# One core, attention and two mixing layers: the DMA order within a head pair laid out by phase, and the E value products moved one slot later

## The chip, the core and the metric

One core of a Trainium2 chip. The metric is the device time of one launch in microseconds (us); the time of the kernel before is the median of three runs. A profiled execution of the same kernel gives the trace.

## What is computed

Three stages follow each other; only the first is touched by the change. The inputs are float32, with 4 batches, 8 heads, 1152 keys, 576 pooled queries and a head dimension of 64.

```python
q_pool = q.reshape(B, H, S // 2, 2, D).mean(axis=3)
scores = scale * np.matmul(q_pool, k.transpose(0, 1, 3, 2))
attn = np.exp(scores - np.max(scores, axis=-1, keepdims=True))
attn = attn / (np.sum(attn, axis=-1, keepdims=True) + 1e-09)
attn_out = np.matmul(attn, v)
# then a gated layer (w_k, w_v, w_r) and a token/channel mixing layer (w_theta, w_tok_*, w_ch)
```

Some weights of the later layers are the bit patterns of 64-bit floats and are turned into pairs of 32-bit numbers by the kernel itself, partly during the attention.

## The kernel before

The 32 heads are handled as 16 pairs (P = 0 to 15). A pair has nine tiles of up to 128 queries against 1152 keys, so there are 144 slots; slot 9P + t belongs to tile t of pair P. The main loop (line 615) runs over the slots. In each slot s it emits, in this order, the entries of `gaps`, the softmax work of tiles s and s+1, the entries of `mids`, the score products and row maxima of tile s+2, the value products planned for s (`run_pv`), and the entries of `sched` (registered by `at`). Each engine and the DMA-issuing queue of SyncE (SP) run what they were given in this order and wait where data are missing; an emission slot is therefore an order and not a time. In one slot, entries of the same list run in the order of their registration: normalisation and block moves first, then `prep_sched`, then the weight conversion.

In pairs 1 to 14 (`quick`) tiles 0 to 3 are transposed in 32x32 blocks by VectorE into `BLK` (line 359), and `move_blocks` (line 361) then puts the blocks in place with 16 DMAs of 32 partitions by 4608 bytes from `BLK` to `E` (line 368), 2.36 MB in a pair. Tiles 4 to 8 are transposed by TensorE (line 334) and copied to `M` (line 391). `pv_part` (line 406) multiplies the values with E (group 0, 18 matmuls, two instructions each) and with M (group 1). Which slots do this is in `shares` (line 340): group 0 in slots 7, 8 and 9 of a pair, group 1 in slots 10, 11 and 12, which are slots 1 to 3 of the next pair.

The other things that go on in a pair's slots:
- `prep_sched` (line 486, tables `PREP1` and `PREP`) prepares the next pair: `kh` and `kl` cut k in two parts on GpSimd (POOL), `km` moves one part by two DMAs of 295 KB (line 255), `q` splits the pooled queries on POOL (`q_split`, line 235), and `lk`, `lq`, `lv` load k, q and v (lines 224, 229, 233; 590 KB for k, for v, and for each half of q).
- `norm1` (line 420) turns the row sums into reciprocals on VectorE, transposes them and stores them to DRAM with four small DMAs (`scr`, line 430); `spread` (line 433) reads them back as a broadcast (`rb`, two DMAs, line 437); `norm2` (line 440) multiplies on POOL. `NORM = (14, 2)` puts norm1 at the end of slot 14, which is slot 5 of the next pair, spread one slot later and norm2 in slot 18.
- The weight conversion (`conv_steps`, line 107): 20 pieces, each a load of 524 KB (line 123), three VectorE steps (`bits`, lines 134, 138 and 142), a few ScalarE and POOL steps, and two stores of 262 KB to DRAM (lines 154, 155). The table `CONV` puts one of the VectorE steps into each of slots 4 to 8 of a pair, and the loads and stores follow seven slots before the first step and three after the last. The pieces rotate through three buffers (`cp`), so the load of one waits for the landing of the stores of the one three before.

SP thus issues everything in one order: the load of a conversion piece stands ahead of the loads of k and q, and these ahead of the 16 block moves. From slot NT = 144 on the later layers run (`mixtures`).

## Time and profile before

| | us |
|---|---|
| median of 3 runs | 1013.45 |
| lowest and highest run | 1011.31, 1016.57 |
| profiled execution, whole | 1010.17 |
| its span, first to last instruction | 1008.4 |
| attention, pairs 1 to 14 (exponential of first tile of pair 1 to that of pair 15) | 446.2 |
| mean granted TensorE clock | 0.978 |

The span is 1.8 us below the profiled execution's time. Times in the rows are us from the start of the span. PE is TensorE, PEld its weight loads, DVE VectorE, ACT ScalarE, SPq the issuing queue of SyncE. In a timeline or a group the bracket or the last column tells how long the engine stood idle before the work and what the profile names as the end of that wait. When several things are waited for, the one that came last is named; the four `scr<-rt` stores are issued right after the 16 block moves, and no matmul reads them, so where a value product is said to have waited for `scr<-rt` it is the E tile that it was waiting for.

### The profile page before, as it was taken

What the parts mean: (1) busy time and instruction counts of PE and PEld (TensorE: products, weight loads), DVE (VectorE), ACT (ScalarE), POOL (GpSimd) and SP (SyncE); (2) the same over time, 40 slices, a digit from 0 to 9 for tenths busy, and PEclk for the clock granted to TensorE, in tenths of its full rate; (3) what the DMA queues carried; (4) which work ended last, traced back from release to release, by engine and by line L of the source; (5) the groups of instructions that cost most, each with busy time, mean ns of one, the idle gap of its engine ahead of it and who ended that gap; (6) DMA issues with size and microseconds to landing.
All of it is one profiled execution on the core that took longest, in us unless ns stands there. A gap on an engine that the chain in (4) does not pass through costs nothing.

```text
span 1008.4 us, 17632 instructions
## 1 busy us (share of the span) xinstructions
PE 935.0 (93%) x6328; PEld 789.0 (78%) x6328; DVE 691.8 (69%) x1006; ACT 517.3 (51%) x1101; POOL 593.0 (59%) x631
## 2 busy tenths in 40 slices
PE   7987997979886988999999999999999999999998
PEld 5765665656564655666779989999999999999998
DVE  6786877876687676877555978888835766466632
ACT  6665654655465455665565555555544434243410
POOL 7846765666565656576622655656646657465731
PEclk9999998999999898999999999999999999999999
DMA  8678978887888788796356333333320701010001
GB/s 213 184 194 220 252 212 238 224 227 212 234 214 219 213 231 229 201 252 165 132 204 215 105 105 91 100 91 106 108 105 7 266 1 48 1 42 7 24 25 48
DMA packets 65848, 150.36 MB, mean 149 GB/s; under 512 B 11936, under 2 KB 31072, under 8 KB 65760
## 3 DMA queue, kind: packets, MB, share of 16 engines
q1 hardware_dynamic: 65760, 149.22, 52.2%
q8 instruction: 50, 0.82, 0.3%
q14 instruction: 38, 0.31, 0.1%
HBM read 81.92 MB, written 24.79 MB: 106 GB/s over the span
## 4 chain that ended last, share of the span: by engine, by line
PE 65%; DMA 13%; DVE 6%; SPq 6%; issue 5%; POOL 3%; ACT 2%; ACTq 0%; POOLq 0%; DVEq 0%
PE ps L1059 11%; PE pv L406 11%; PE sc L291 9%; PE ps L811 9%; PE ps L792 8%; DMA E<-blk 5%; PE ps L1078 5%; PE ps L1005 5%; SPq L368 4%; PE sc L334 3%; PE ps L761 3%; DMA scr<-rt 2%; DMA qn<-qT 2%; DVE m L312 2%; DMA a<-wk 1%
## 5 line engine op out<-in xcount | busy, mean ns | idle before, releaser
L291 PE MATMUL sc<-kt,q 128*128 128x384 f32 (+1 forms) x864 | 204.8, 359 | 25.0 <-DVE M L391 20.3
L324 ACT ACTIVATE e<-sc,m 128x1152 f32<-128x1152 f32 x144 | 176.3, 1225 | 90.0 <-DVE m L312 87.2
L312 DVE TENSOR_REDUCE m<-sc 128x1 f32<-128x1152 f32 x138 | 187.0, 1355 | 49.7 <-PE sc L291 42.9
L291 PEld LDWEIGHTS sc<-kt,q 128*128 128x128 f32 (+1 forms) x864 | 143.1, 188 | 59.2 <-DVE M L391 33.1
L1059 PE MATMUL ps<-b,a 128*128 128x288 f32 x816 | 111.3, 296 | 0.0
L1059 PEld LDWEIGHTS ps<-b,a 128*128 128x128 f32 x816 | 109.4, 189 | 0.6
L406 PE MATMUL pv<-E,vn 128*64 128x256 f32 x576 | 78.9, 413 | 31.6 <-DMA scr<-rt 27.7
L792 PE MATMUL ps<-x,a 128*128 128x288 f32 x768 | 105.2, 298 | 2.3 <-DVE xt L816 2.3
L792 PEld LDWEIGHTS ps<-x,a 128*128 128x128 f32 x768 | 103.8, 191 | 2.6 <-DVE xt L816 2.6
L811 PE MATMUL ps<-k,b 128*128 128x288 f32 x768 | 103.6, 295 | 0.0
L811 PEld LDWEIGHTS ps<-k,b 128*128 128x128 f32 x768 | 102.2, 188 | 0.3
L391 DVE COPY M<-sc 128x384 f32<-128x384 f32 x77 | 41.8, 545 | 72.5 <-PE sc L334 72.4
L201 POOL TENSOR_TENSOR kt<-kn,kh 64x576 fp32r<-64x576 f32 (+1 forms) x64 | 90.1, 1427 | 2.2
L334 PEld LDWEIGHTS sc<-idn,e 128*128 128x128 f32 x528 | 61.3, 147 | 36.5 <-ACT e L324 18.4
L334 PE MATMUL sc<-idn,e 128*128 128x128 f32 x528 | 80.0, 290 | 8.2 <-ACT e L324 7.1
L406 PE MATMUL pv<-M,vn 128*64 128x320 f32 x576 | 87.5, 441 | 0.0
L406 PEld LDWEIGHTS pv<-E,vn 128*64 128x64 f32 x576 | 41.2, 145 | 58.5 <-issue 43.9
L391 ACT COPY M<-sc 128x384 f32<-128x384 f32 x83 | 39.4, 480 | 80.9 <-PE sc L334 80.4
L359 DVE STREAM_TRANSPOSE blk<-e 128x1152 f32<-128x1152 f32 x56 | 76.5, 1367 | 0.0
L779 POOL TENSOR_TENSOR k<-h,k 128x288 fp32r<-128x288 f32 x64 | 56.7, 895 | 28.3 <-ACT k L778 27.0
L150 POOL TENSOR_TENSOR cv<-cv 128x512 fp32r<-128x512 f32 x20 | 25.6, 1278 | 77.1 <-ACT cv L146 63.5
L406 PEld LDWEIGHTS pv<-M,vn 128*64 128x64 f32 x576 | 37.4, 136 | 36.1 <-issue 11.2
(136 smaller groups left out, 1658.3 us busy)
## 6 DMA issues: line engine op xcount, KB each, us to landing
E<-blk SPq DMA_DIRECT2D x224, 144.0 KB
qn<-qT SPq DMA_DIRECT2D x60, 288.0 KB
vn<-vP SPq DMA_DIRECT2D x16, 576.0 KB
kt<-kh SPq DMA_DIRECT2D x31, 288.0 KB
kn<-kT SPq DMA_DIRECT2D x15, 576.0 KB
b<-wtk SPq DMA_DIRECT2D x9, 576.0 KB
rb<-scr SPq DMA_DIRECT2D x32, 144.0 KB
out<-xt SPq DMA_DIRECT2D x32, 144.0 KB
```

The lines of the kernel that those rows point to most:

```text
L201: engines[e].tensor_tensor(out, x, hi.bitcast(F32), ALU.subtract)
L291: r = pe.matmul(sc[0:m, c, 0:384], lhsT=x, rhs=k[:, 384 * c:384 * c + 384], start=(i == 0), stop=(i == len(ops) - 1),)
L312: r = dve.tensor_reduce(m, scs[n][:, :, 0:384], axis=AX.XY, op=ALU.max, negate=True)
L324: r = act.activation(e, sc[:, :, 0:384], AF.Exp, bias=m, scale=1.0, accum_out=rss[P][:, t:t + 1])
L334: r = pe.transpose(ps[:, 128 * j:128 * j + 128], es_[n][:, c, 128 * j:128 * j + 128], idn)
L359: dve.transpose(out, es_[n].rearrange("p a b -> p (a b)").rearrange("p (k m i) -> p k m i", k=KT, m=4))
L391: r = (act.copy if e == "act" else dve.tensor_copy)(out, ps)
L406: pe.matmul(out, lhsT=vns[P][:, h, j], rhs=e, start=(x == 0), stop=(x == KT - 1))
L779: pool.tensor_tensor(q[:, 1], h, q[:, 0].bitcast(F32), ALU.subtract)
L792: pe.matmul(ps, lhsT=WK[k, f // 4][:, w, 128 * (f % 4):128 * (f % 4) + 128], rhs=x[k][:, c], start=(k == 0 and n == 0), stop=(k == 3 and n ...
L811: pe.matmul(pss[d], lhsT=WV[f][:, w, 128 * d:128 * d + 128], rhs=k2[f][:, c], start=(f == 0 and n == 0), stop=(f == 7 and n == 2))
L1059: pe.matmul(pss[d], lhsT=zs[j][z][:, 128 * d:128 * d + 128], rhs=WTK[min(j, 8)][:, w, cs], start=(m == 0 and n == 0), stop=(m == 8 and n = ...
```

## The change

It redistributes work over slots; no arithmetic is removed.
- `shares`: E products in slots 8 (four key tiles) and 9 (five) in place of 7, 8 and 9 (three each); in pair 14 in slots 7 (two) and 8 (seven).
- Normalisation: `NORM = 9`. The two small steps on the sums go to POOL (`norm0`, slot 9), the reciprocal and the transpose to the end of slot 10 (VectorE), the four stores to the middle of slot 11, the read back to the middle of slot 12, the multiplication to the end of slot 14. Slots 9 to 14 are slots 0 to 5 of the next pair. Stores and read back now stand ahead of that pair's block moves.
- Preparation: `km` from slot 0 to the end of slot 1, `lk` from 2 to 1, first half of `lq` from the end of slot 2 to the middle of 3, second half from 7 to 8, `lv` from 7 to 8.
- Conversion: pieces are tied to pairs 1 to 13, two in odd pairs and one in even ones. Loads at the end of the slot before the pair, the VectorE steps in slots 4, 5, 6 and, for the second piece, 6, 7, 8; stores in the middle of slot 2 of the next pair.

```diff
-NORM = (14, 2)
+NORM = 9
-PREP = ((0, 0, 'kh', 'pool'), (0, 2, 'km'), (0, 2, 'q', 0), (2, 2, 'lk'), (2, 2, 'lq', 0), (2, 1, 'kl', 'pool', 0, 0), (2, 2, 'kl', 'pool', 0, 1), (3, 2, 'q', 1), (5, 1, 'kl', 'pool', 1, 0), (5, 2, 'kl', 'pool', 1, 1), (7, 2, 'lq', 1), (16, 2, 'lv'))
-CONV = ((4, 1), (5, 1), (6, 1), (7, 1), (8, 1))
+PREP = ((0, 0, 'kh', 'pool'), (1, 2, 'km'), (0, 2, 'q', 0), (1, 2, 'lk'), (3, 1, 'lq', 0), (2, 1, 'kl', 'pool', 0, 0), (2, 2, 'kl', 'pool', 0, 1), (3, 2, 'q', 1), (5, 1, 'kl', 'pool', 1, 0), (5, 2, 'kl', 'pool', 1, 1), (8, 2, 'lq', 1), (17, 2, 'lv'))
+BITS = ((4, 5, 6), (6, 7, 8))
...
             if P == NP - 2:
-                return ((7, 5), (8, 4)), ((9, 5), (11, 4))
+                return ((7, 2), (8, 7)), ((9, 5), (11, 4))
...
-            return ((7, 3), (8, 3), (9, 3)), ((10, 3), (11, 3), (12, 3))
+            return ((8, 4), (9, 5)), ((10, 3), (11, 3), (12, 3))
...
+        def norm0(P):
+            rs, r2 = rss.pop(P), R2[P % 2]
+            pool.tensor_scalar(r2[:, 0:KT], rs[:, 0:KT], 1e-9, 1.0, op0=ALU.add, op1=ALU.mult)
+            pool.tensor_scalar(r2[0:64, KT:KT + 1], r2[64:128, 4:5], 1.0, 1.0, op0=ALU.mult, op1=ALU.mult)
...
-            dve.tensor_scalar(r2[:, 0:KT], rs[:, 0:KT], 1e-9, 1.0, op0=ALU.add, op1=ALU.mult)
-            dve.reciprocal(r2[:, 0:KT], r2[:, 0:KT])
-            dve.tensor_copy(r2[0:64, KT:KT + 1], r2[64:128, 4:5])
+            dve.reciprocal(r2[:, 0:KT + 1], r2[:, 0:KT + 1])
             dve.transpose(rt, r2)
...
+        def norm3(P):
+            scr, rt = scrs.pop(P)
             for b4 in range(4):
                 sp.dma_start(out=scr[:, 32 * b4:32 * b4 + 32], in_=rt[32 * b4:32 * b4 + KT + 1, :])
-            at(last_slot + 3 if P == NP - 1 else P * KT + NORM[0] + 1, spread, P, scr)
+            (at if P == NP - 1 else at_mid)(last_slot + 3 if P == NP - 1 else P * KT + NORM + 3, spread, P, scr)
...
-            o, hook = NORM
-            (at_gap, at_mid, at)[hook](min(P * KT + o, NT), norm1, P)
-            at(min(P * KT + o, NT) + (4 if P < NP - 1 else 6), norm2, P)
+            at(P * KT + NORM, norm0, P)
+            at(min(P * KT + NORM + 1, NT), norm1, P)
+            at_mid(min(P * KT + NORM + 2, NT + 1), norm3, P)
+            at(P * KT + NORM + (5 if P < NP - 1 else 6), norm2, P)
...
+        for P in range(1, NP - 2):
+            base = P * KT
+            for bits, (i, piece) in zip(BITS[:1 + P % 2], pieces):
...
+                at(base - 1, load)
+                at_mid(base + 2, mag)
+                at(base + 2, clamp)
+                for o, step in zip(bits, cuts):
+                    at_mid(base + o, step)
+                at_mid(base + KT, hi)
+                at(base + KT, lo)
+                at_mid(base + KT + 2, store)
```

## Rows read from the trace of the kernel before

**Rows 1.** The page's second part: busy tenths of TensorE in 40 slices of 25.2 us.

```profile
PE   7987997979886988999999999999999999999998
```

**Rows 2.** Stretches, pairs 1, 5, 9, 12, 14: us; busy PE, PEld, DVE, ACT, POOL; PEclk; DMA; GB/s.

```profile
38.60:67.20 28.60, 25.03 (x163) 18.16 (x160) 24.61 (x30) 17.16 (x31) 16.43 (x16) 1.00 0.63 159
...
166.90:196.00 29.10, 27.12 (x179) 18.92 (x177) 24.48 (x28) 18.69 (x35) 20.25 (x20) 1.00 0.85 240
...
295.30:332.10 36.80, 28.61 (x175) 19.59 (x174) 24.81 (x27) 18.07 (x35) 19.45 (x19) 0.89 0.82 202
...
397.90:427.70 29.80, 27.56 (x179) 19.33 (x178) 24.39 (x28) 17.51 (x34) 18.53 (x17) 0.98 0.80 218
...
455.90:484.80 28.90, 27.71 (x186) 19.23 (x183) 20.52 (x23) 16.57 (x32) 15.80 (x15) 1.00 0.63 157
```

**Rows 3.** Groups by line, whole span: busy, mean ns | idle before, what ended it.

```profile
L406 PE MATMUL pv<-E,vn 128*64 128x256 f32 x576 | 78.9, 413 | 31.6 <-DMA scr<-rt 27.7 <-DMA E<-blk 3.9
```

**Rows 4.** Timeline of PE around slot 7 of pairs 9 and 12.

```profile
328.01 2.83 PE L406 MATMUL pv<-E,vn 128*64 128x256 f32 x12 [5.95 <-DMA scr<-rt]
...
422.13 0.62 PE L291 MATMUL sc<-kt,q 128*128 128x384 f32 x2 [1.55 <-DVE M L391]
...
425.29 1.52 PE L406 MATMUL pv<-E,vn 128*64 128x256 f32 x12
426.73 0.88 PE L334 MATMUL sc<-idn,e 128*128 128x128 f32 x6
...
428.92 1.52 PE L406 MATMUL pv<-E,vn 128*64 128x256 f32 x12
```

**Rows 5.** Timeline of SP's issues in pair 9, up to its block moves.

```profile
299.35 0.54 SPq L155 DMA_DIRECT2D wv<-cv  x1
308.95 0.33 SPq L123 DMA_DIRECT2D cv<-wv  x1
309.33 0.43 SPq L224 DMA_DIRECT2D kn<-kT  x1
309.86 1.13 SPq L229 DMA_DIRECT2D qn<-qT  x2
311.10 13.45 SPq L368 DMA_DIRECT2D E<-blk  x16
```

**Rows 6.** The same in pair 12: block moves, store of sums, read back.

```profile
411.61 10.99 SPq L368 DMA_DIRECT2D E<-blk  x16
422.70 1.58 SPq L430 DMA_DIRECT2D scr<-rt  x4
425.37 1.12 SPq L437 DMA_DIRECT2D rb<-scr  x2
```

**Rows 7.** Waits, us in total, times, longest: three of SP's queue, one of TensorE.

```profile
SPq L368 <- DVE blk L359: 33.1, 7, 10.6
...
SPq L123 <- DMA wk<-cv: 22.7, 4, 8.6
SPq L437 <- DMA scr<-rt: 21.1, 21, 2.4
...
PE pv L406 <- DMA scr<-rt: 27.7, 9, 6.0
```

**Rows 8.** Timeline of VectorE in pair 7.

```profile
238.71 1.36 DVE L312 TENSOR_REDUCE m<-sc 128x1 f32<-128x1152 f32 x1
...
243.54 1.37 DVE L359 STREAM_TRANSPOSE blk<-e 128x1152 f32<-128x1152 f32 x1
...
250.96 0.89 DVE L142 SCALAR_TENSOR_TENSOR cv<-cv 128x512 uint32<-128x512 uint32 x1
...
253.29 0.22 DVE L425 RECIPROCAL r<-r 128x9 f32<-128x9 f32 x1
...
253.72 0.21 DVE L427 STREAM_TRANSPOSE rt<-r 128x32 f32<-128x32 f32 x1
```

**Rows 9.** One stretch of pair 12 ahead of its block moves, columns as in rows 2.

```profile
402.00:406.00 4.00, 4.00 (x28) 2.55 (x28) 3.93 (x4) 2.37 (x5) 3.66 (x5) 1.00 1.02 271
```

More of the change, by code (lines that the diff above doesn't have):

```diff
@@ L29 @@
 HALF = 288
-CFIRST = 4
 WARM = 16
@@ L216, in attention @@
         for t in RS + R2:
-            pool.memset(t, 0.0)
+            pool.memset(t, 1.0)
         for b in range(NB):
@@ L418, in attention @@
         rbs = {}
+        scrs = {}
+        def norm0(P):
+            rs, r2 = rss.pop(P), R2[P % 2]
+            pool.tensor_scalar(r2[:, 0:KT], rs[:, 0:KT], 1e-9, 1.0, op0=ALU.add, op1=ALU.mult)
+            pool.tensor_scalar(r2[0:64, KT:KT + 1], r2[64:128, 4:5], 1.0, 1.0, op0=ALU.mult, op1=ALU.mult)
         def norm1(P):
-            rs = rss.pop(P)
             r2 = R2[P % 2]
             rt = sm.tile([128, 32], F32, tag="rt", name="rt")
-            dve.tensor_scalar(r2[:, 0:KT], rs[:, 0:KT], 1e-9, 1.0, op0=ALU.add, op1=ALU.mult)
-            dve.reciprocal(r2[:, 0:KT], r2[:, 0:KT])
-            dve.tensor_copy(r2[0:64, KT:KT + 1], r2[64:128, 4:5])
+            dve.reciprocal(r2[:, 0:KT + 1], r2[:, 0:KT + 1])
             dve.transpose(rt, r2)
             scr = dram.tile([KT + 1, 128], F32, tag="scr", name="scr")
+            scrs[P] = scr, rt
+        def norm3(P):
+            scr, rt = scrs.pop(P)
             for b4 in range(4):
                 sp.dma_start(out=scr[:, 32 * b4:32 * b4 + 32], in_=rt[32 * b4:32 * b4 + KT + 1, :])
-            at(last_slot + 3 if P == NP - 1 else P * KT + NORM[0] + 1, spread, P, scr)
+            (at if P == NP - 1 else at_mid)(last_slot + 3 if P == NP - 1 else P * KT + NORM + 3, spread, P, scr)
         def spread(P, scr):
@@ L588, in attention @@
             prep_sched(P)
-        places = [(KT * i + o, hook) for i in range(NP - 1) for o, hook in CONV]
-        for i, piece in enumerate(first):
-            load, mag, clamp, *bits, hi, lo, store = conv_steps(lambda i: cp.tile([128, 1536], F32R, tag="cv", name="cv"), piece, i, engines[CLO], pool)
-            mine = places[CFIRST + 3 * i:CFIRST + 3 * i + 3]
-            a, z = mine[0][0], mine[-1][0]
-            at(a - 7, load)
-            at_mid(a - 2, mag)
-            at(a - 2, clamp)
-            for (o, hook), step in zip(mine, bits):
-                (at_gap, at_mid, at)[hook](o, step)
-            at_mid(z + 1, hi)
-            at(z + 1, lo)
-            at(z + 3, store)
+        pieces = iter(enumerate(first))
+        for P in range(1, NP - 2):
+            base = P * KT
+            for bits, (i, piece) in zip(BITS[:1 + P % 2], pieces):
+                load, mag, clamp, *cuts, hi, lo, store = conv_steps(lambda i: cp.tile([128, 1536], F32R, tag="cv", name="cv"), piece, i, engines[CLO], pool)
+                at(base - 1, load)
[6 more added lines that the diff above has]
+                at_mid(base + KT + 2, store)
+        assert next(pieces, None) is None
         def load_wr():
@@ L625, in attention @@
                         tfill(s, c)
-                    for c in (1, 2):
-                        tcopy(s, c)
+                    tcopy(s, 1)
+                    tcopy(s, 2)
                     sexp(s + 1)
```

## The prediction

> **What bounds the kernel now.** I read the page's slices first, then a table with one stretch for each head pair, then the groups by line, and last the timelines around the longest stall. TensorE is at nine tenths or more from slice 17 (403 us) to the last but one, and loses time before that [rows 1], so what can be won lies in the attention. There the pairs differ: pairs 1, 5 and 12 take 28.6, 29.1 and 29.8 us, pair 9 takes 36.8, with a granted clock of 0.89 where pair 5 has 1.00 [rows 2]. Pairs 1 to 14 go from 38.60 to 484.80 [rows 2], 446.2 us or 31.9 us each.
>
> The groups name the cause: the value products on E have 31.6 us of idle TensorE ahead of them [rows 3], nearly all in nine pairs [rows 7], where slot 7 makes its first product on E. Pair 9 is the worst: TensorE stands for 5.95 us, and the first twelve instructions then take 2.83 us where pair 12 needs 1.52 [rows 4], so the stop is paid again at a lower clock. The matmul waits for the last block move. In pair 9 SP issued a store at 299.35 and then nothing until 308.95, when the load of a conversion piece could go [rows 5]; such loads waited for the landing of the stores that free their buffer, 22.7 us for one weight alone [rows 7]. The loads of k and q stood behind that load and left right ahead of the block moves, 1.7 MB within 2.2 us [rows 5]. From the first block move at 311.10 [rows 5] to the product at 328.01 [rows 4] it took 16.9 us. In pair 12 SP was free before the last transpose, so the queue had time to drain, as in the seven cases where SP waited for the transposes [rows 7]; from 411.61 [rows 6] to 425.29 [rows 4] it took 13.7 us, and there was no stall worth naming.
>
> **Ceiling.** The three pairs without a stall that have conversion steps average (28.6 + 29.1 + 29.8) / 3 = 29.2 us [rows 2]. Fourteen such pairs take 409, that is 37 us less than 446: the 31.6 us of waiting, and about 6 for the low clock and the delays that a stall drags along.
>
> **The later products.** Group 0 keeps its 36 instructions, so its TensorE time is unchanged. Its first use of E moves from slot 7 to slot 8: in pair 12 these are 425.29 and 428.92 [rows 4], 3.6 us apart, of which 1.44 is slot 7's own product (425.29 to 426.73) that goes. So the deadline moves by 2.2 us, to 13.7 + 2.2 = 15.9 us after the blocks are ready. Slot 7 loses work that covered the wait for the next exponential. That bubble is bounded by nothing and by the whole 1.44; I take 0.2 for each of 13 pairs, 3 us: the transposes of slot 8 start at 426.73, with no idle time after the product [rows 4], so TensorE and not the exponential held them back. Slots 8 and 9 get 0.5 and 1.0 us more of products; slot 9 has only block transposes on VectorE, and TensorE sets the pace there.
>
> **The new order on SP.** The conversion loads leave a slot before the pair, their buffers long free, so the 9.6 us hole of pair 9 [rows 5] has nothing to come from. `km` and `lk` pass from beside the block moves to behind the previous pair's loads. What now stands ahead of the block moves is the four stores of the sums, which wait for `norm1`, then two or four conversion stores, half of q, and the read back, which waits for the landing of the stores of the sums. `norm1` runs behind the maximum of tile 3, in pair 7 from 240.07 (238.71 + 1.36 [rows 8]), and takes 0.43 (0.22 + 0.21 [rows 8]). The blocks are ready at 244.91 (243.54 + 1.37 [rows 8]), so SP has 4.4 us. It needs 1.58 for the sums [rows 6], 0.5 each for two or four stores (the 0.54 of pair 9), 1.13 for half of q [rows 5] and 1.12 for the read back [rows 6]: 4.9 or 6.0 us. The block moves start 0.5 us late after an even number of pieces and 1.6 us after two, where pair 9 was about 3 late.
>
> How long they then take depends on what still flows. The stores (0.5 or 1.0 MB), half of q (0.6) and the read back (0.3) are 1.4 or 1.9 MB, issued over 4.9 or 6.0 us; at the 271 GB/s of pair 12 ahead of its moves [rows 9] 0.1 to 0.3 MB are left, and with some latency perhaps 0.5. Bounds: 13.7 us as in pair 12 with a drained queue, 16.9 as in pair 9. I take 14.5, nearer to the drained end, because the same bytes are spread over more than twice the time. E then lands 15.0 or 16.1 us after the blocks against a deadline of 15.9: a residual of 0 or 0.2, with the bounds 0 and (17.4 to 18.5) - 15.9 = 1.5 to 2.6, on average 2 in 13 pairs, 26 us. I take 6 us, for pairs whose queue is fuller than the mean.
>
> The Trainium skill speaks against this place for the sums. "DMA: Bandwidth & Descriptors", section "Anatomy of one DMA", says that a DMA has a fixed cost of some 2 us, mostly the receipt of the write and heaviest for HBM, and that any wait is held on the issuing sequencer. By it 2 us of return would stand before the block moves in each pair, an estimate of 26 us if the block moves sat on their deadline. The trace is milder: in pair 12 the last store of sums was issued by 424.28 and the read back left at 425.37, 1.1 us later [rows 6], SP's waits for it total 21.1 us in 21 [rows 7], and in the new order the stores and half of q take 2.2 us or more between the two.
>
> **The rest.** On VectorE `norm1` loses the step on the sums and a copy, leaves the crowded slot 5, and puts 0.43 us into slot 1. At worst 0.43 x 14 = 6 us; at best the 1.55 us gap of slot 7, where TensorE waits for a copy behind VectorE's conversion steps [rows 4], shrinks by half, 11 us. Conversion: odd pairs now have two steps in slot 6, a second one costing up to 0.89 [rows 8], 6 us in seven pairs; even pairs have none in slots 7 and 8. I set these two against each other, at nothing. On POOL `norm0` adds two steps on ten columns or less, by the nearest row 0.22 each [rows 8], and POOL is busy 20 of 29 us [rows 2]. The splitting of q is queued behind it and waits for the last exponential of the pair; that is 6 us ahead of SP's need of the freed q buffer. `norm2` moves forward four slots, behind a read back that lands before it. VectorE's reciprocal now waits for POOL; behind it stand the block transposes. Load of v and the other half of q move one slot later, to right behind the block moves, where nothing waits for them for a pair. After the attention nothing moves except the last pair's stores of sums, behind loads that were there before; nothing.
>
> **Sum.** 1010.2 - 37 + 3 (bubble) + 6 (residual) = 982 us. The profiled run is 3 us below the median of the three, whose spread is about 5 us; I make no correction. Bounds: all hidden with a lighter slot 5, 1010 - 37 - 11 = 962; the long flight in every pair and the worst of VectorE, 1010 - 37 + 3 + 26 + 6 = 1008. A figure within 0.5%, 5 us, can't be told from no change here.
>
> **Rivals.**
> 1. *The transfers are the bound.* A pair moves 2.4 MB for E, 1.2 for q, 0.6 each for k, v and `km`, 0.3 for the read back and on average 1.5 for the conversion (20 x 1.05 / 14), 7.1 in all; at pair 9's 202 GB/s [rows 2] this takes 35 us, at pair 5's 240 it fits into 29.6. If the new order reaches only 225, about halfway, a pair takes 31.5, fourteen 441, and the kernel 1005. For it: the DMA share is 0.80 to 0.85 in slow and quick pairs alike [rows 2]. Against it: pair 5 moves all of it in 29.1. The Trainium skill ("DMA: Bandwidth & Descriptors", "Specifications") puts the fabric's ceiling at 435 GB/s; by that an estimate of 16 us for a pair would leave nothing late and the sum would be 976, but the rows show the engines full at 271 GB/s [rows 9].
> 2. *The block moves fly as long as in pair 9.* Residual 26, so 1002.
> 3. *Slower: the read back becomes the stall.* The stores of sums wait in the DMA rings behind the loads of v, q, k and the conversion, 2.9 to 3.4 MB issued behind the previous block moves. If these still flow, the read back is held on SP with all 16 block moves behind it. Each us of this beyond the deadline costs 13 us, so it decides from about 2.4 us over (31.6 / 13); at 5 us late it is 1010 - 37 + 3 + 65 = 1041. Against it: at 271 GB/s 3.4 MB need 12.5 us, and from the landing of E to the stores of the sums there are about that many.
> 4. *It doesn't do what it says*: E's wait is another transfer's, and the time stays at 1010. The chain of waits and the dates of the block moves speak against it.
>
> **How the numbers follow.** Forecast (968 to 996) 0.72; rival 2 0.12; rival 1 0.05; rival 3 0.07; rival 4 0.04. Faster by over 0.5% (below 1008) comes from the first two and most of the third, 0.87; same 0.06; slower 0.07. Range: the forecast's own from 966, up to 1003 to take in rival 2.
>
> **What would show it.** Right: idle time ahead of the E products falls from 31.6 to under 10 us; every pair between 28.5 and 30.5 us at a clock of 0.98 or more; SP waits for `blk` before most block moves or issues them within 2 us of the last transpose; waits for `wk<-cv` at line 123 vanish. Wrong: a wait of SP for `scr` of over 2 us ahead of the block moves (rival 3), block moves on time but 16 us and more in flight (rival 2), or the stall turning up at VectorE's block transposes, which can't start before the old blocks have left.

## The result and the profile after

| | before | after |
|---|---|---|
| median, us | 1012.93 (4 runs) | 975.65 (4 runs, 973.63 to 977.85) |
| ratio, 95% interval | | 0.963 (0.959 to 0.966) |
| profiled execution, us | 1010.17 | 973.63 |
| its span, us | 1008.4 | 971.8 |
| TensorE busy / idle in the span, us | 935.0 / 73.4 | 922.3 / 49.5 |
| pairs 1 to 14, us | 446.2 | 410.5 (29.3 each, 28.0 to 30.6) |
| idle TensorE before the E products, us | 31.6 | 9.4 |
| mean granted TensorE clock | 0.978 | 0.996 |

The forecast was 982 us with a range of 966 to 1003. The kernel became 37 us faster, and nearly all of it came from the pairs: 446.2 - 410.5 = 35.7.

The page's second part of the kernel after (TensorE, its granted clock, the DMA engines, in 40 slices of 24.3 us):

```profile
PE   7989999889999899998999899999999999999998
PEclk9999999999999999999999999999999999999999
DMA  8698999999999999976473333333402501010001
```

Of the first 16 slices four read seven and one six before [rows 1]; now one reads seven, the first, and the clock reads nine throughout. The DMA line is the new thing: the engines are at nine tenths or more in nearly every slice of the attention. Stretches of the kernel after (pairs 5 and 9, then one long stretch of the attention; columns as in rows 2):

```profile
153.90:183.20 29.30, 26.85 (x176) 18.80 (x175) 24.38 (x26) 18.43 (x34) 20.41 (x22) 1.00 0.90 242
271.20:301.80 30.60, 27.22 (x177) 19.10 (x176) 24.70 (x27) 18.32 (x34) 20.54 (x22) 1.00 1.01 262
80.00:404.00 324.00, 296.06 (x1915) 206.00 (x1915) 266.65 (x269) 201.12 (x364) 226.23 (x231) 1.00 0.97 246
```

A long stretch of the attention in the kernel before:

```profile
80.00:440.00 360.00, 307.95 (x1913) 213.50 (x1913) 265.51 (x297) 199.24 (x366) 227.40 (x212) 0.95 0.84 225
```

Pair 9 took 36.8 us at a clock of 0.89 [rows 2] and now takes 30.6 at 1.00. Over the long stretch the DMA share went from 0.84 to 0.97 and the rate from 225 to 246 GB/s: about the same bytes in less time, and the engines are seldom without work.

Groups by line of the kernel after (busy, mean ns | idle before, what ended it):

```profile
L290 PE MATMUL sc<-kt,q 128*128 128x384 f32 (+1 forms) x864 | 201.9, 357 | 16.2 <-DVE M L390 11.7 <-DMA kt<-kh 3.6 <-DVE E L390 0.4
...
L333 PE MATMUL sc<-idn,e 128*128 128x128 f32 x528 | 77.2, 283 | 17.1 <-ACT e L323 16.0
L405 PE MATMUL pv<-E,vn 128*64 128x256 f32 x576 | 69.5, 385 | 9.4 <-DMA E<-blk 7.7 <-DMA vn<-vP 1.5 <-PE sc L290 0.2
```

The same groups of the kernel before, without the one of rows 3:

```profile
L291 PE MATMUL sc<-kt,q 128*128 128x384 f32 (+1 forms) x864 | 204.8, 359 | 25.0 <-DVE M L391 20.3 <-DMA kt<-kh 3.6 <-DVE E L391 0.5
...
L334 PE MATMUL sc<-idn,e 128*128 128x128 f32 x528 | 80.0, 290 | 8.2 <-ACT e L324 7.1
```

Three things are read here. The wait of the E products fell by 22.2 us, and the 576 instructions themselves take 385 ns where they took 413 [rows 3]. The scores wait 8.6 us less for VectorE's copies to `M`. The transposes wait 8.9 us more for the exponential. The last two nearly cancel.

Two causes lie behind the shorter E products. The TensorE time of one pair's 36 instructions before, in pair 12 without a stall and in pair 9 behind one (us, busy PE, clock, DMA, GB/s):

```profile
424.00:440.00 16.00, 4.55 (x36) 1.00 0.77 230
326.00:345.00 19.00, 5.86 (x36) 0.79 0.63 167
```

The same after, in pair 9:

```profile
300.00:316.00 16.00, 4.33 (x36) 1.00 0.84 239
```

The stall's lower clock cost 1.31 us in pair 9. But at a clock of 1.00 the instructions also take 0.22 us less than before, because they now come in two batches in place of three (4.55 and 4.33; in one batch, in all_in_9 below, it is 4.11).

SP's timeline around the block moves of pair 8 (start, us, line, transfer, count):

```profile
252.35 1.42 SPq L437 DMA_DIRECT2D scr<-rt  x4
253.87 0.34 SPq L153 DMA_DIRECT2D wk<-cv  x1
...
255.28 1.39 SPq L154 DMA_DIRECT2D wk<-cv  x1
256.72 1.14 SPq L228 DMA_DIRECT2D qn<-qT  x2
257.95 1.18 SPq L444 DMA_DIRECT2D rb<-scr  x2
259.24 10.09 SPq L367 DMA_DIRECT2D E<-blk  x16
269.43 0.53 SPq L232 DMA_DIRECT2D vn<-vP  x1
...
273.59 0.58 SPq L223 DMA_DIRECT2D kn<-kT  x1
```

Sums, conversion stores, half of q and the read back leave without a hole, then the 16 moves in 10.1 us (13.45 in pair 9 before, [rows 5]), then everything that can wait. A wait of POOL in the kernel after (us in total, times, longest):

```profile
POOL r L423 <- ACT e L323: 52.1, 15, 6.3
```

The first of SP's own waits that lies in the attention:

```profile
SPq L437 <- DVE rt L430: 120.7, 16, 14.0
```

SP now stands 120.7 us in 16 waits for the transposed sums. In this time the rings empty themselves of the loads issued behind the last moves (by rings I mean the transfers that SP has issued and that are not done yet; the trace shows them only through the DMA share, which in pair 8 is 0.99 and 1.04 from 244 to 252 us, while SP stands, and 0.59 in the next 4 us). The wait is not free, though: what stands behind it leaves late enough that the block moves start 1.9 us after the last transpose on average, and sums_late below shows the kernel without it. The waits for `wk<-cv` at the load of a piece [rows 7] are gone. Pair 9, where the stall was worst, from the last block transpose over the block moves to the first E product:

```profile
285.21 1.37 DVE L358 STREAM_TRANSPOSE blk<-e 128x1152 f32<-128x1152 f32 x1
...
287.40 10.19 SPq L367 DMA_DIRECT2D E<-blk  x16
...
302.44 1.95 PE L405 MATMUL pv<-E,vn 128*64 128x256 f32 x16
```

The blocks are ready at 286.58 (285.21 + 1.37), SP issues 0.8 us later, and TensorE comes to the product after 15.9 us with no wait. Of pairs 2 to 13, those with an odd number have the stores of one conversion piece ahead of their moves, and only pair 5 waits (0.5 us); those with an even number have the stores of two and wait 0.2 to 1.8 us. Pair 14, with its own slots, waits 1.7.

### The profile page after: what moved, and what is told of

The parts are those of the page before. It is cut to its first block, busy times and chain, and to the rows that moved or that the text cites. A ratio compares the mean times of both kernels' runs of the same rounds, so it can differ in the third digit from the quotient of the medians.

```text
span 971.8 us, 17617 instructions
## 1 busy us (share of the span) xinstructions
PE 922.3 (95%) x6328; PEld 780.9 (80%) x6328; DVE 698.1 (72%) x974; ACT 519.8 (53%) x1101; POOL 597.7 (62%) x663
## 4 chain that ended last, share of the span: by engine, by line
PE 73%; DVE 9%; DMA 6%; SPq 5%; issue 3%; ACT 3%; POOL 0%; ACTq 0%; DVEq 0%; POOLq 0%
PE pv L405 15%; PE ps L1068 12%; PE sc L290 10%; PE ps L820 9%; PE ps L801 9%; PE ps L1087 5%; PE ps L1014 5%; SPq L367 5%; DMA E<-blk 4%; PE ps L770 3%; DVE m L311 3%; PE sc L333 3%; ACT e L323 2%; DVE M L390 1%; DMA kt<-kh 1%
## 5 line engine op out<-in xcount | busy, mean ns | idle before, releaser
L290 PE MATMUL sc<-kt,q 128*128 128x384 f32 (+1 forms) x864 | 201.9, 357 | 16.2 <-DVE M L390 11.7
L333 PEld LDWEIGHTS sc<-idn,e 128*128 128x128 f32 x528 | 57.2, 142 | 46.5 <-ACT e L323 36.1
L333 PE MATMUL sc<-idn,e 128*128 128x128 f32 x528 | 77.2, 283 | 17.1 <-ACT e L323 16.0
L405 PE MATMUL pv<-E,vn 128*64 128x256 f32 x576 | 69.5, 385 | 9.4 <-DMA E<-blk 7.7
L804 DVE TENSOR_TENSOR h<-h 128x288 f32<-128x288 f32 x64 | 38.3, 604 | 29.1 <-ACT h L803 28.8
L390 DVE COPY M<-sc 128x384 f32<-128x384 f32 x77 | 41.9, 547 | 20.4 <-PE sc L333 20.3
L1044 POOL TENSOR_TENSOR q<-t,q 128x256 f32<-128x256 f32 x32 | 24.5, 785 | 49.0 <-ACT q L1034 49.0
```

The source lines that it names most:

```text
L290: r = pe.matmul(sc[0:m, c, 0:384], lhsT=x, rhs=k[:, 384 * c:384 * c + 384], start=(i == 0), stop=(i == len(ops) - 1),)
L333: r = pe.transpose(ps[:, 128 * j:128 * j + 128], es_[n][:, c, 128 * j:128 * j + 128], idn)
L390: r = (act.copy if e == "act" else dve.tensor_copy)(out, ps)
L405: pe.matmul(out, lhsT=vns[P][:, h, j], rhs=e, start=(x == 0), stop=(x == KT - 1))
```

## The experiments

My theory after the result: the gain comes from *what stands ahead of the block moves on SP*. The later slots give 2.2 us of tolerance, and the order lets the blocks land within it, or little beyond; each alone should give only a part. Rivals: the order does it all; one moved part (the sums, the conversion, q) does it; or the DMA engines are full, so that only bytes count. "Behind" and "ahead" mean the place relative to the 16 block moves in SP's order.

In this table the delay is from the end of the fourth block transpose to the first block move, and the issue the time from the first move to the end of the last, both means of pairs 2 to 13 from the timelines; idle is TensorE's time before the E products, and blk VectorE's before the block transposes, from the groups by line.

| kernel | us | ratio (95%) | idle | blk | delay | issue |
|---|---|---|---|---|---|---|
| before | 1012.9 | 1 | 31.6 | 0.0 | 0.8 | 12.1 |
| after | 975.7 | 0.963 (0.959 to 0.966) | 9.4 | 0.3 | 1.9 | 10.4 |
| shares_only | 1005.7 | 0.995 (0.992 to 0.998) | 29.1 | 17.1 | 2.2 | 12.9 |
| order_only | 1014.9 | 1.003 (1.000 to 1.006) | 38.4 | 0.0 | 1.1 | 10.4 |
| sums_behind | 991.8 | 0.979 (0.973 to 0.985) | 14.4 | 4.3 | 1.3 | 12.6 |
| conv_old | 984.2 | 0.970 (0.965 to 0.976) | 17.0 | 5.5 | 3.0 | 10.3 |
| q_behind | 980.8 | 0.969 (0.963 to 0.975) | 4.6 | 0.2 | 2.7 | 10.3 |
| q_first | 987.3 | 0.975 (0.970 to 0.980) | 16.1 | 6.1 | 3.8 | 10.4 |
| v_twice | 983.0 | 0.973 (0.966 to 0.979) | 10.4 | 1.3 | 2.2 | 10.5 |
| q_twice | 1000.9 | 0.989 (0.984 to 0.994) | 23.6 | 11.2 | 1.8 | 11.6 |
| stores_behind | 1014.3 | 1.002 (0.998 to 1.006) | 36.9 | 21.8 | 5.5 | 10.3 |
| sums_late | 967.8 | 0.957 (0.950 to 0.964) | 0.6 | 0.0 | 0.06 | 11.0 |
| all_in_9 | 974.1 | 0.963 (0.957 to 0.969) | 3.6 | 1.9 | 2.3 | 10.5 |
| late_sums_old_slots | 969.1 | 0.960 (0.957 to 0.963) | 10.3 | 0.0 | 0.06 | 10.7 |

### Each half alone: shares_only and order_only

The kernel before with the new slots of the value products, and the kernel after with the old ones:

```diff
 # shares_only, on the kernel before
-                return ((7, 5), (8, 4)), ((9, 5), (11, 4))
+                return ((7, 2), (8, 7)), ((9, 5), (11, 4))
-            return ((7, 3), (8, 3), (9, 3)), ((10, 3), (11, 3), (12, 3))
+            return ((8, 4), (9, 5)), ((10, 3), (11, 3), (12, 3))
 # order_only, on the kernel after: the same four lines, the other way
```

> The kernel before with one edit: the E products in slots 8 and 9 (pair 14: 7 and 8); every DMA stays where it was. Theory (landing of the block moves against a deadline, both halves of the change needed): the deadline moves by 2.2 us, so of the nine stalls only what lies above 2.2 us stays, 1.5 + 2.4 + 2.7 + 1.9 + 3.8 + 1.3 = 13.6 us of idle TensorE ahead of the E products, and about half of the time at the low clock goes: 992 us, between 985 and 1000. Rival, the DMA order does it all: 1008 or more, idle time still near 30 us. Rival, the later product does it all: 980 or less.

> The changed kernel with the E products back in slots 7, 8 and 9; its DMA order stays. Theory: the blocks land 15 to 17.4 us after they are ready, the deadline is 13.7 again, so some 2 us of stall in 13 pairs, 26 us of idle TensorE instead of 9.4, with part of it at the low clock: 1000 us, between 990 and 1006. Rival, the DMA order does it all: 980 or less. Rival, the later product does it all: 1010.

The slots alone give 5 us (0.995 of before, timed in the same series), the order alone none (1014.9, interval 1.000 to 1.006), and together they give 37. My numbers for both halves were too optimistic; the rivals' 1008 and 1010 were closer. The group of E products in shares_only:

```profile
L406 PE MATMUL pv<-E,vn 128*64 128x256 f32 x576 | 76.7, 414 | 29.1 <-DMA scr<-rt 27.8 <-DMA E<-blk 1.3
```

A wait of VectorE in shares_only:

```profile
DVE blk L359 <- DMA scr<-rt: 17.1, 7, 4.6
```

The group of E products in order_only:

```profile
L405 PE MATMUL pv<-E,vn 128*64 128x256 f32 x576 | 79.3, 415 | 38.4 <-DMA E<-blk 20.9 <-DMA vn<-vP 15.8 <-issue 1.8
```

The load of v (`vn<-vP`) that is named here is issued right behind the 16 moves; as with `scr<-rt`, I take it for the E tile. The transposes of TensorE in shares_only:

```profile
L334 PE MATMUL sc<-idn,e 128*128 128x128 f32 x528 | 76.5, 281 | 12.3 <-ACT e L324 11.2
```

The same in order_only:

```profile
L333 PE MATMUL sc<-idn,e 128*128 128x128 f32 x528 | 81.7, 294 | 12.4 <-ACT e L323 11.4
```

With the old order the blocks don't land at a fixed time: in the pairs that wait in shares_only, the product starts 16.2 to 22.2 us after the blocks are ready, because the moves start up to 6.0 us late and are issued over 12.9. In the worst of them the blocks leave so late that the next pair's block transposes wait for the buffer (17.1 us, 7 times; none in before), which puts that pair back as well. So the tolerance is eaten: TensorE may wait 2.2 us longer for E, but nothing made the blocks keep to it. The same second wait returns in the later runs whose moves land latest (column blk). With the new order and the old slots the landing is even (14.4 to 17.4 us after the blocks are ready in pairs 2 to 13, where it is 13.6 to 19.8 in those of them that wait in before), but the deadline is some 13 us, so every pair waits, 1.0 to 4.3 us. An even landing is worth something only if it is even on the right side of the deadline: a pair pays for the excess, and gets nothing back for being early.

### One moved part at a time: sums_behind, conv_old, q_behind, q_first

In sums_behind stores and read back of the sums follow directly behind the block moves:

```diff
-            (at if P == NP - 1 else at_mid)(last_slot + 3 if P == NP - 1 else P * KT + NORM + 3, spread, P, scr)
+            (at if P == NP - 1 else at_mid)(last_slot + 3 if P == NP - 1 else P * KT + NORM + (3 if P == NP - 2 else 6), spread, P, scr)
-            at_mid(min(P * KT + NORM + 2, NT + 1), norm3, P)
+            at_mid(min(P * KT + NORM + (2 if P >= NP - 2 else 5), NT + 1), norm3, P)
-            at(P * KT + NORM + (5 if P < NP - 1 else 6), norm2, P)
+            at(P * KT + NORM + (6 if P == NP - 1 else 5 if P == NP - 2 else 11), norm2, P)
```

> The changed kernel with one part undone: the stores of the sums at slot 14 and the read back at slot 15, that is behind the block moves of the next pair, and the multiplication at slot 20 (pairs 0 to 13). Theory: the four stores with their wait for VectorE are what holds the block moves back by 0.8 to 4.1 us after the last transpose; without them the moves leave within 0.1 us of it in nearly every pair, the queue has drained, the flight is 13 to 14 us and the idle time ahead of the E products falls from 9.4 to 2 us or less: 968 us, between 965 and 972. Rival, the transfers are the bound: the flight grows by what the start gains, idle time still 7 us or more: 974 to 978. Rival, the read back behind the block moves holds up POOL: slower than 978.

991.8, 16 us slower than after: my theory, in the form "the fewer DMAs ahead of the moves, the better", fell here. SP's timeline in pair 8:

```profile
265.92 13.49 SPq L367 DMA_DIRECT2D E<-blk  x16
279.45 2.12 SPq L437 DMA_DIRECT2D scr<-rt  x4
283.66 1.12 SPq L444 DMA_DIRECT2D rb<-scr  x2
284.88 0.54 SPq L232 DMA_DIRECT2D vn<-vP  x1
```

A stretch at the moves and one in the hole, columns as in rows 2:

```profile
266.00:270.00 4.00, 3.92 (x26) 3.13 (x24) 3.41 (x5) 3.38 (x6) 3.66 (x5) 1.00 1.04 367
282.00:286.00 4.00, 2.99 (x14) 1.90 (x16) 1.38 (x1) 0.00 (x0) 2.66 (x2) 0.50 0.13 48
```

The read back doesn't leave until the stores of the sums have landed (21.2 us in 23 waits of SP). It stands directly behind them, and the rings empty themselves while SP waits: 2.1 us (281.57 to 283.66) with a DMA share of 0.13 for the stretch and, this being the pair with the longest stop before the E products (4.5 us), TensorE at the lower clock of 1.2 GHz (0.50). The loads held behind it then leave closer to the next pair's moves, which are issued over 12.6 us; that the one makes the other longer is read from this, not shown by itself. Over the long stretch (80 to 404 us) the DMA share is 0.89 where after has 0.97. The Trainium skill ("DMA: Bandwidth & Descriptors", "Anatomy of one DMA — SWDGE (gpsimd) path") puts some 2 us on a DMA, most of it the receipt of the write; it says this of DMAs that GpSimd issues. The 2.1 us here, with drained rings and from SyncE, are of that size; the prediction used the figure without saying where it was measured.

conv_old puts the conversion back to its old places (loads seven slots before the first step, stores three after the last), on the kernel after:

> The changed kernel with the conversion pieces in their old places (one VectorE step in each of slots 4 to 8, load seven slots before, stores three slots after). Theory: the hole of SP at the load that waits for the landing of stores comes back ahead of the block moves in a third to a half of the pairs, their start slips by 1 to 3 us there, idle time ahead of the E products 15 to 25 us: 985 us, between 980 and 995. Rival, the conversion's place doesn't matter as long as the sums and loads have theirs: 974 to 978.

984.2, as expected, with 17.0 us of idle time. One of its waits:

```profile
SPq L123 <- DMA wk<-cv: 16.9, 5, 6.6
```

The loads that wait for their buffers are back, together with those for two other weights (24.1 us), and the moves start up to 6.3 us late. This part of the change is worth some 9 us, though its interval just touches that of after.

q_behind and q_first move the load of the first half of q behind the moves, or ahead of the sums:

```diff
 # q_behind: (3, 1, 'lq', 0) -> (4, 2, 'lq', 0)
 # q_first:  (3, 1, 'lq', 0) -> (1, 2, 'lq', 0)
```

> The changed kernel with the first half of the load of q at the end of slot 4 in place of the middle of slot 3: 590 KB pass from ahead of the block moves to right behind them. Theory 1 (what stands ahead of the moves in the rings sets when the blocks land): the moves leave 1.1 us sooner and fly about 2 us shorter (590 KB at 240 GB/s), the idle time ahead of the E products falls from 9.4 to 2 us or less: 967 us, between 963 and 971. Theory 2 (the DMA engines are nearly full, at a share of 0.95 in the attention, and any order that keeps them full gives the same): 973 to 979.

> The changed kernel with the same 590 KB at the end of slot 1, behind the load of k and ahead of the stores of the sums. Theory 1: the 4 us ahead of the last block transpose, where the share of the DMA engines is 0.5 to 0.7, take them up, so the blocks land some 2 us sooner: 967 to 972. Theory 2: 973 to 979. Rival: the stores of the sums now stand behind 3.5 to 4 MB in the rings, land later, and the read back holds up the block moves on SP: 980 or more, with SP's wait for the stores of the sums ahead of most moves.

q_behind was a miss: 980.8 where I expected 967, 5 us above after (the intervals overlap). The idle time of the E products did fall, to 4.6 us, and the pairs gained nothing from it. What changed is that POOL now waits for q:

```profile
POOL qn L238 <- DMA qn<-qT: 54.7, 13, 6.4
```

The conversion's steps stand behind that on POOL, their stores leave late, and these stand ahead of the moves, which start up to 5.7 us late. But the E products hardly wait for them; what grew is the scores' wait for VectorE's copies (15.8 us, 11.7 in after), that of the transposes (17.7 and 16.0) and TensorE's busy time (926.7 and 922.3). How POOL's wait leads there isn't shown. A load that looks as if it could wait was one that another engine's queue needed. In q_first (987.3, as the rival said) the read back has no load to hide behind:

```profile
SPq L444 <- DMA scr<-rt: 15.9, 20, 3.2
```

In the kernel after that wait is 1.2 us in all (4 times). The half of q between stores and read back is not just in the way; it covers part of the return of the stores.

### Bytes or place: v_twice and q_twice

Both load 459 KB in each pair into a tile that nobody reads (a useless load is added, nothing is left out), behind the moves with the load of v or ahead of them with that of q:

```diff
+        dump = ring.tile([128, 896], F32, name="dump")
 # in load_v if P > 1, or in load_q if P > 2 and h == 0:
+                sp.dma_start(out=dump, in_=kT[P][:, 0:896])
```

> The changed kernel with a useless load of 459 KB per pair (pairs 2 to 15, into a tile that nothing reads) next to the load of v, right behind the block moves. Theory 1 (only what stands ahead of the moves costs): the gap before the next moves, about 2 us of free engine time per pair, takes it up: 976 to 983. Theory 2 (the engines are full): 459 KB at 240 GB/s are 1.9 us in each of 14 pairs, up to 27 us in all: 990 to 1003.

> The same useless load of 459 KB (pairs 3 to 15) next to the first half of q, ahead of the block moves. Theory 1: each flight is 1.9 us longer in pairs that are at or near their deadline, 13 x 1.9 = 25 us and some time at the low clock on top: 1000 to 1012, clearly more than the same bytes behind the moves. Theory 2: 990 to 1003, the same as behind the moves.

Behind the moves the extra bytes cost 7 us, ahead of them 25. The theory of places had both, the first at the edge of its range; theory 2 had the second too, but said the two would be the same. In q_twice the landing is late enough for the second wait as well (11.2 us). The long stretch in v_twice:

```profile
80.00:404.00 324.00, 293.39 (x1897) 204.57 (x1896) 265.99 (x265) 198.32 (x360) 225.93 (x230) 1.00 0.98 258
```

v_twice moves 258 GB/s where after moves 246. So the engines had room for more bytes at a share of 0.97, and a high share is not by itself a bound. The prediction had read a share of 1.02 at 271 GB/s [rows 9] as engines that are full; with 367 GB/s at 1.04 in sums_behind that figure is no limit.

### Making room ahead of the moves in two ways: stores_behind and sums_late

stores_behind puts the conversion stores directly behind the moves. sums_late takes sums_behind and moves the read back further, to slot 17, behind the loads of v, q and the conversion:

```diff
 # stores_behind
-                at_mid(base + KT + 2, store)
+                at(base + KT + 3, store)
 # sums_late: norm3 and norm2 as in sums_behind, and for P < NP - 2
+            at(P * KT + NORM + 8, spread, P, scr)
```

> The changed kernel with the conversion's stores (0.5 or 1.0 MB, two or four DMAs) right behind the block moves instead of ahead of them. Theory 1 (bytes and issues ahead of the moves set their landing): moves start within 0.5 us of the last transpose, flight 13 us, idle time ahead of the E products 0 to 3 us, no load of q delayed: 967 us, between 963 and 971. Rival: what passes behind the moves is still in the rings when the next stores of the sums go, the read back is held and the moves start 2 us and more late, as in q_first: 976 or more.

> As sums_behind (the stores of the sums behind the block moves), but the read back is issued behind the loads of v, q and the conversion (slot 17) instead of ahead of them. Theory 1 (sums_behind lost because SP held the loads back while it waited for the sums, with nothing else in the rings, and the loads then flew ahead of the next block moves): the hole behind the moves closes, share of the DMA engines 0.93 or more where sums_behind has 0.88, the time falls from 992 back to 970 to 978. Theory 2 (the wait for VectorE ahead of the moves is itself of use, since it lets the rings drain): the moves are still issued over 12 to 13 us into full rings, idle time ahead of the E products stays at 12 us or more, 985 to 995.

stores_behind gives 1014.3 where I expected 967: the whole gain is gone, and only the rival had the direction. SP's timeline in pair 8:

```profile
274.02 2.35 SPq L228 DMA_DIRECT2D qn<-qT  x2
281.16 1.09 SPq L444 DMA_DIRECT2D rb<-scr  x2
282.35 10.07 SPq L367 DMA_DIRECT2D E<-blk  x16
```

SP's wait for the stores of the sums:

```profile
SPq L444 <- DMA scr<-rt: 49.8, 21, 5.3
```

The stores of the sums land late, and SP stands at the read back from 276.37 to 281.16 with all 16 moves behind it. Two things changed at once: the conversion stores were issued, with the loads, ahead of the next sums, and they no longer stand between the sums and the read back, where their issue covered part of the return. The run doesn't tell how much each does. The moves start 5.5 us late on average, 9.5 at most, and the next pair's block transposes wait too (21.8 us in all). This is rival 3 of the prediction, made real by moving one line.

sums_late gives 967.8, 0.957 of before, the lowest median of the study and below the 970 to 978 of theory 1. SP's timeline in pair 8:

```profile
257.45 10.71 SPq L367 DMA_DIRECT2D E<-blk  x16
268.21 1.63 SPq L437 DMA_DIRECT2D scr<-rt  x4
...
272.75 1.23 SPq L444 DMA_DIRECT2D rb<-scr  x2
```

The group of E products in sums_late:

```profile
L405 PE MATMUL pv<-E,vn 128*64 128x256 f32 x576 | 69.4, 385 | 0.6 <-DMA scr<-rt 0.6
```

SP's wait for the block transposes there:

```profile
SPq L367 <- DVE blk L358: 54.5, 14, 8.4
```

SP's wait at the read back in sums_behind:

```profile
SPq L444 <- DMA scr<-rt: 21.2, 23, 2.1
```

The same in sums_late:

```profile
SPq L444 <- DMA scr<-rt: 0.9, 2, 0.5
```

The long stretch in sums_late:

```profile
80.00:404.00 324.00, 302.79 (x1956) 209.96 (x1953) 269.53 (x273) 203.95 (x368) 235.12 (x240) 0.99 0.94 252
```

All 14 groups of moves start 0.06 us after the last transpose, because SP is there before it every time, and 0.6 us of idle time is left. Between sums_behind and sums_late only the place of the read back differs, and it is worth 24 us: issued behind the loads, 2.9 us after the last store of the sums in pair 8, it finds them landed and SP hardly waits; directly behind the stores, SP waits and the rings empty (DMA share of the long stretch 0.94 and 0.89). The pairs went from 410.5 in after to 401.5, about the 8.8 us of idle time that after still had (9.4 - 0.6). After and sums_late were timed in separate series; the highest run of one (971.5) is below the lowest of the other (973.6), but the intervals of their ratios touch (0.950 to 0.964, 0.959 to 0.966).

### The slots again: all_in_9 and late_sums_old_slots

```diff
 # all_in_9, on the kernel after
-            return ((8, 4), (9, 5)), ((10, 3), (11, 3), (12, 3))
+            return ((9, 9),), ((10, 3), (11, 3), (12, 3))
 # late_sums_old_slots: sums_late with the shares of order_only
```

> The changed kernel with all nine key tiles of the E products in slot 9 (pairs 1 to 13), one slot later again. Theory 1: the deadline moves by another 2 to 3 us, the waits for E vanish but for pair 14 (under 2 us in all), and what comes in their place is idle time of TensorE in slot 8, ahead of the transposes, where it has nothing to do while the exponential runs: 972 to 980, no gain. Rival: with the blocks always there the pairs run at 28.5 us: 965 to 970. Rival: the products now hold the row maxima of the next tiles, VectorE falls behind: 985 or more.

> sums_late with the E products back in slots 7, 8 and 9. Theory 1 (landing against a deadline; in sums_late the moves leave on time in every pair, and their landing is known only to be under 14 to 16 us): the deadline is 13.7 us again, flights of 13 to 15.5 us leave a wait of up to 2 us in most pairs, 10 to 20 us in all with some time at the low clock: 985 us, between 977 and 995. Rival, with the moves on time the later products are not needed: 964 to 971, idle time ahead of the E products under 4 us. Rival, the place of the products is worth as much as with the other order (order_only was 39 us over the changed kernel): 1003 or more.

all_in_9 (974.1, as expected) can't be told from after. Its groups:

```profile
L290 PE MATMUL sc<-kt,q 128*128 128x384 f32 (+1 forms) x864 | 202.7, 358 | 23.5 <-DVE M L390 11.9 <-DMA kt<-kh 6.0 <-issue 4.7
...
L405 PE MATMUL pv<-E,vn 128*64 128x256 f32 x576 | 68.7, 391 | 3.6 <-DMA E<-blk 3.6
```

The products wait 5.8 us less and the scores 7.3 more: a bubble for a wait. late_sums_old_slots (969.1) can't be told from sums_late either. Its groups:

```profile
L333 PE MATMUL sc<-idn,e 128*128 128x128 f32 x528 | 77.8, 284 | 12.5 <-ACT e L323 11.4
...
L405 PE MATMUL pv<-E,vn 128*64 128x256 f32 x576 | 73.1, 390 | 10.3 <-DMA scr<-rt 9.3 <-DMA E<-blk 1.0
```

The E products wait 10.3 us again (the rival that fits the time had said under 4), but the transposes 4.6 less than in sums_late (17.1 there, as in after) and the scores 3.9 less (14.0 and 17.9). I had expected 985. The later slots are worth 39 us with the sums ahead of the moves (1014.9 to 975.7) and about one with the sums behind (969.1 to 967.8): they buy 2.2 us of tolerance, and moves that leave on time, landing 13.8 us after the blocks on average in the pairs that wait, hardly need it.

## Why the prediction was right, step by step

- **What bounds it, and the ceiling.** Right: the E products waited for block moves behind loads. The 37 us were forecast as the gap to clean pairs at 409, and pairs 1 to 14 now take 410.5; but 409 is no floor, since in sums_late they take 401.5. The waits sat in ten pairs, not nine: pair 11's 3.5 us go by the name `E<-blk`. The step that was mis-sized is the low clock: the sum gave the 31.6 us of waiting and about 6 for low clock and drag. TensorE's busy time, for the same 6328 matmuls, fell by 935.0 - 922.3 = 12.7 us. Of this, 0.22 us in 13 pairs, 2.9 us, is not the clock but the products in two batches in place of three: "its TensorE time is unchanged" was wrong by that much. The other 9.8 us came with the clock's rise from 0.978 to 0.996, some 4 more than I booked. Together they are most of the 8.6 us between the 982.2 of the sum and the profiled 973.6. The 2.83 us against 1.52 of one first product [rows 4] was no row to multiply by nine: four pairs show 2.83, one 2.33, one 2.03, and the other eight of pairs 1 to 14 show 1.52, 6.6 us in all. The rest is in the scores and transposes that follow.
- **Deadline.** Right: 15.9 us was the sum, and the pairs of 3 to 13 that don't wait take 15.65 to 15.88. The old one was nearer 13.2 than 13.7 (order_only, where all pairs wait), so it moved by 2.6 us. That it would hardly help alone was not in the prediction; shares_only showed it.
- **Start and flight of the block moves.** I had 0.5 us late behind one piece (the "even number" there is a slip) and 1.6 behind two, and 14.5 in flight. Measured 1.6 and 2.1, 1.9 on average (0.8 to 1.7 in most pairs, 3.6 and 2.5 in pairs 6 and 8, 4.1 in pair 5, where the conversion stores left 1.5 and 0.9 us after SP was free) and 14.5 in flight over the seven of pairs 2 to 13 that wait, 12.4 to 15.6. Which pairs wait was right in kind: those behind two pieces. The residual was 6 and is 9.4. What I had not seen is that the moves start later than before on average (0.8 there): the order brings nothing at the start. It shortens the issue (12.1 to 10.4) and the flight (15.6 us in the ten of these pairs that waited before), and takes away the landings at 18.7 and 19.8 us.
- **The bubble of slot 7.** The transposes now wait 8.9 us more for the exponential (7.1 to 16.0), where I had 3. The two halves split this: 11.2 in shares_only, 11.4 in order_only. So the moved products bring 4.1 to 4.6, some 0.3 us for each pair where I took 0.2, and late_sums_old_slots gives 4.6 back with the old slots. The other 4.3 to 4.8 came with the order and stand in no term of the sum.
- **VectorE.** I set relief of slot 5 and the doubled step against each other, at nothing; the scores' wait for copies fell by 8.6 (20.3 to 11.7), within the 11 that I had as best case. It came with the order (10.9 in order_only, 19.5 in shares_only). In conv_old, where the conversion's steps are back in their old places, it is 7.0, so the doubled steps may cost some 5 of the 6 that I feared and the relief be larger than my best case; what else differs in that run is not separated. In sum, idle time fell by 73.4 - 49.5 = 23.9 where I had 31.6 - 3 - 6 = 22.6: a bubble too small by 6, a relief missing by 8.6 and a residual too small by 3.4 nearly cancel. That this came out right is partly luck.
- **The rest at nothing.** Held: POOL's `norm0` waits 52.1 us for the last exponential, and VectorE, which needs its result, lists no wait for it.
- **Rivals.** Transfers as the bound: no, 258 GB/s were reached in v_twice. The 976 that is worked out there for nothing being late is near the measured time by luck, since 9.4 us of waits were left. Long flight: no in after, yes in shares_only, where it takes the gain away. The read back as stall: not in after (1.2 us), but real as a mechanism. In stores_behind the moves were 5.5 us late and the time came back to before's; I had priced each us beyond the deadline at 13, and 5 us late at 1041. That took a late start for a late landing: the moves start 3.6 us later than in after (5.5 - 1.9) but are 12.9 us in flight where they wait, 14.5 in after, and the E products wait 27.5 us more (36.9 - 9.4), 2.1 in each of 13 pairs. For this the kernel takes 39 us more, so a us beyond the deadline costs 18 rather than 13; the lower clock and the second wait come on top. And the argument by which I ruled it out, that the rings have some 12 us to drain, didn't hold once the conversion stores passed behind the moves.
- **Not foreseen.** That the place I took as given, sums ahead of the moves, was not the best one. What I had against it was the return of the stores, and in after this is covered. What it does cost is 1.9 us of delay in each pair, 8 us in all by the two medians.
- **The signs.** Idle time ahead of the E products under 10 us and no wait for `wk<-cv` came as named. The pairs take 28.0 to 30.6 us, just wider than 28.5 to 30.5, and in pairs 5, 6 and 8 the moves start more than 2 us late.

Open: I haven't separated how much of the 9 us of conv_old is the loads and how much the VectorE steps. And sums_late wasn't tried together with another place for q or the conversion; its remaining idle time stands at the transposes (17.1 us) and the scores (17.9), which no order of DMAs showed a way to remove. All runs issue from SP; whether the moves land sooner when a second engine issues part of them wasn't tried.

## What to carry over

On a queue that issues in order, sort by what each wait does to the transfers, not by what seems urgent. In this kernel a wait cost little while other transfers were still running and nothing urgent stood behind it, and much when the DMA engines ran empty or the urgent transfers stood behind it; a store that is read back wants other transfers between the two. Judge a transfer by its deadline and not by its mean, since a pair that lands early gives nothing back: evening out the landings and moving the deadline brought 37 us together, 5 by the deadline alone and none by the order alone. With stores and read back of the sums behind the moves the later slots are hardly needed (969.1 without, 967.8 with them). Price a stall with the slower clock that follows it, from the same instruction's duration with and without, and count the places where it shows.

## What the runs showed of the hardware

- The same 6328 matmuls kept TensorE busy for 935.0 us at a mean granted clock of 0.978 and 922.3 at 0.996: 22.2 us less waiting for E (31.6 - 9.4) came with 12.7 us less time for the same work, 2.9 of them from E products in fewer batches.
- The 36 value products of a pair kept TensorE busy for 4.55 us in three batches (before, pair 12), 4.33 in two (after, pair 9) and 4.11 in one (all_in_9, in 12 of 13 pairs), at a granted clock of 1.00: each break cost 0.22 us.
- Issuing 16 block moves took SP 10.1 us in pair 8 of after, and 13.5 in pair 9 before, where 1.7 MB of loads had left in the 2.2 us ahead [rows 5], and in pair 8 of sums_behind. Issue time alone is two thirds of the 15 us until the blocks have landed.
- At a DMA share of 0.97 the rate was 246 GB/s, at 0.98 258 with 459 KB more in each pair (v_twice), at 1.04 367 in the first 4 us of one pair's moves (sums_behind). Here the share told that the engines held work, not how much more they could take.
- From the last store of sums to its read back SP waited 2.1 us at a DMA share of 0.13 (sums_behind), up to 5.3 us in stores_behind, where conversion stores and loads had been issued ahead of the sums, and 0.9 us in all where loads were issued in between (sums_late).
